# Wider token blocks, and a state product in whole float32

## The chip, the cores and the metric

The kernel runs on one core of one Trainium2 chip. The metric is the device time of one execution in microseconds (us). A core has five engines with queues of their own: TensorE (PE in the profile, its weight loads PEld) multiplies matrices into PSUM; VectorE (DVE), ScalarE (ACT) and GpSimd (POOL) work element by element; SyncE (SP) issues most of the transfers (DMAs).

## The reference

Attention with a decaying state, and a feed-forward part behind it with softplus. Inputs are float32 and random; four sequences of 768 tokens, eight heads of 64, so the feed-forward part sees 3072 tokens of 512 features, with 2048 hidden columns.

```python
for t in range(S):
    state = gamma[None, :, None, None] * state + np.einsum('bhd,bhe->bhde', k[:, :, t], v[:, :, t])
    y[:, :, t] = scale * np.einsum('bhd,bhde->bhe', q[:, :, t], state)
...
x = np.ascontiguousarray(attn_out.transpose(0, 2, 1, 3)).reshape(B * S, H * D)
h = x @ w_in
g = np.maximum(h, 0.0) + np.log1p(np.exp(-np.abs(h)))
return (g @ w_out).astype(np.float32)
```

## The kernel before

**Precision.** The code multiplies operands in two forms: float32r, one record a product in the profile, and whole float32, which the profile shows as two records a product. For most products it splits an operand into a high and a low float32r part and adds three products (high x high, high x low, low x high) in PSUM. The names end in h and l: `xh`, `xl`, `gh`, `gl`, `kh`, `kl`, and `vhl` for both parts of v.

**Attention.** It is cut into 48 units: 24 chunks of 128 tokens, each with two halves of four heads. What a unit does is spread over ticks: the dictionary `PARTS` (line 264) says at which tick after the unit's start each part runs, and a new unit begins every four ticks. `load_unit` (six ticks ahead) fetches k, q, v through SP; `decay` (two ahead) scales q and v on POOL; `operands` (0) transposes k and q on TensorE (lines 125, 127) and splits k, q and v; `scores` (2) multiplies them; `new_state` (3) multiplies k by v into `pp` and adds that to the state `td` (lines 202, 204), unless the chunk is the last of its sequence; `stack_and_outputs` (5) copies the state and makes the outputs `yp`, then `xh` and `xl`. The first ten units (`n < WHOLE`) use whole float32 products, the others the split form. For `pp` that is one product for each head on line 191 (four heads, 64 stationary and 64 moving columns), or two on lines 195 (128 moving columns) and 196. TensorE's attention results share three PSUM banks in rotation (`ps_a`, tag `a`).

**Feed-forward.** Blocks of `T` = 256 tokens. A step takes one block and two of the 16 column tiles of 128: `hidden` (lines 279 to 288) makes `hp` with 2 x 12 products of 256 columns; `softplus_1` and `softplus_2` turn that into `gh` and `gl` with two operations on VectorE, two on ScalarE and one on POOL; `second`, two steps later (`LAG`), multiplies by `w_out` into one accumulator for each 128 tokens (`acc0`, `acc1`), three products of 512 columns for each column tile and accumulator. A block has eight steps, and its accumulators are copied out at its end.

**Order.** The main loop (line 410) runs over the steps: hidden products of step s, some ticks of attention, output products of step s - 2, some more ticks. `plan` spreads the ticks that the next block needs evenly over the steps of the present one. The first blocks are special (`turns`): five steps of block 0, all of block 1, then the rest of block 0, while the weights are still being fetched and converted (`convert_weights`, with PSUM tile `wp` and buffer `w`); block 2's ticks run in the five steps ahead of it. Tile sizes its pools from the names and tags, and a planner may set independent instructions of one engine in another order than the code's.

Of the kernel before, what the change touches and what calls it, by code (L numbers as in the profile page):

```python
# [18 lines left out]
C = 128  # L19
T = 256  # L20
AHEAD = 2
# [9 lines left out]
def decay_attention_then_softplus_ffn(ctx: ExitStack, tc: tile.TileContext, q, k, v, w_in, w_out, qtab, vtab, gtab, out):  # L31
# [5 lines left out]
    NF = DF // P  # L37
    NP = NF // 2
    HH = H // 2
    NJ = HH // 2  # L40
    NT = T // P
# [4 lines left out]
    wts = ctx.enter_context(tc.tile_pool(name="wts", bufs=2))  # L46
    ps_h = ctx.enter_context(tc.tile_pool(name="ps_h", bufs=2, space=bass.MemoryType.PSUM))
    ps_o = ctx.enter_context(tc.tile_pool(name="ps_o", bufs=1, space=bass.MemoryType.PSUM))
    ps_w = ctx.enter_context(tc.tile_pool(name="ps_w", bufs=1, space=bass.MemoryType.PSUM))
    ps_a = ctx.enter_context(tc.tile_pool(name="ps_a", bufs=3, space=bass.MemoryType.PSUM))  # L50
# [23 lines left out]
    def convert_weights(f):  # L74
# [21 lines left out]
    loads, live, state, xs = {}, {}, {}, {}  # L96
    lo, up = slice(0, D), slice(D, P)
# [22 lines left out]
    def operands(n):  # L120
# [5 lines left out]
        for j in range(NJ):  # L126
            nc.tensor.transpose(tp[:, 1, j, :], qn[:, 2 * j:2 * j + 2, :], ident)  # L127
        if n < WHOLE:
            kw = attn.tile([P, NJ, C], F32, name="kw", tag="kh")
# [4 lines left out]
            live[n] = [(kw, qw), kn, vn]  # L134
            return
# [11 lines left out]
        nc.vector.tensor_tensor(vhl[:, :, 1, :], vn, vhl[:, :, 0, :].bitcast(F32), op=ALU.subtract)  # L147
        kh = kl = None
        if c < NC - 1:
            kh = attn.tile([P, HH, D], F32R, name="kh", tag="kh")  # L150
            kl = attn.tile([P, HH, D], F32R, name="kl")
            nc.scalar.copy(kh, kn)
            nc.vector.tensor_tensor(kl, kn, kh.bitcast(F32), op=ALU.subtract)
        live[n] = [kq, vhl, kh, kl]

# [26 lines left out]
    def new_state(n):  # L182
        b, c, hf = units[n]
        live[n].append(state[hf][0] if c else None)
        if c == NC - 1:
            return
        pp = ps_a.tile([D, HH, 2, D], F32, name="pp", tag="a")
        if n < WHOLE:
            kn, vn = live[n][1:3]
            for h in range(HH):  # L190
                nc.tensor.matmul(pp[:, h, 0, :], lhsT=kn[:, h, :], rhs=vn[:, h, :], start=True, stop=True)
        else:
            vhl, kh, kl = live[n][1:4]
            for h in range(HH):
                nc.tensor.matmul(pp[:, h], lhsT=kh[:, h, :], rhs=vhl[:, h], start=True, stop=False)  # L195
                nc.tensor.matmul(pp[:, h, 0, :], lhsT=kl[:, h, :], rhs=vhl[:, h, 0, :], start=False, stop=True)
        if c == 0:
            td = attn.tile([D, HH, D], F32, name=f"td{hf}")
            nc.vector.tensor_copy(td, pp[:, :, 0, :])
# [27 lines left out]
    def outputs(n):  # L227
        b, c, hf = units[n]
        kq, *rest, st = live.pop(n)
        i, off = divmod((n // 2) * C, T)  # L230
        if i not in xs:
            xs[i] = [ffn.tile([P, ND, T], F32R, name=nm) for nm in ("xh", "xl")]
        xh, xl = xs[i]
        yp = ps_a.tile([D, 2, NJ, C], F32, name="yp", tag="a")
        for j in range(NJ):
            for par in range(2):
# [7 lines left out]
                if n < WHOLE:  # L244
                    kn, vn, a = rest
                    nc.tensor.matmul(o, lhsT=vn[:, h, :], rhs=a[:, h, :], start=c == 0, stop=True)  # L246
                else:
                    vhl, kh, kl, ah, al = rest
                    nc.tensor.matmul(o, lhsT=vhl[:, h, 0, :], rhs=ah[:, h, :], start=c == 0, stop=False)  # L249
# [18 lines left out]
    per_block = PERIOD * 2 * NT  # L268

# [9 lines left out]
    def hidden(s):  # L279
        i, p = steps[s]  # L280
# [10 lines left out]
    def softplus_1(s):  # L291
        sp = sps[s] = ffn.tile([P, 2, T], F32, name="sp")
        nc.vector.tensor_scalar(sp.bitcast(U32), hps[s].bitcast(U32), 0x80000000, None, op0=ALU.bitwise_or)  # L293
        nc.scalar.activation(sp, sp, AF.Softplus)  # L294

    def softplus_2(s):
        g = sps[s]
        nc.vector.scalar_tensor_tensor(g, hps.pop(s), 0.0, g, op0=ALU.max, op1=ALU.add)  # L298
        gh = ffn.tile([P, 2, T], F32R, name="gh")
        nc.scalar.copy(gh, g)  # L300
        gl = ffn.tile([P, 2, T], F32R, name="gl")
        nc.gpsimd.tensor_tensor(gl, sps.pop(s), gh.bitcast(F32), op=ALU.subtract)  # L302
        gs[s] = gh, gl

    def second(s):
        i, p = steps[s]
        gh, gl = gs.pop(s)
        begins = s == 0 or steps[s - 1][0] != i
        ends = s + 1 == len(steps) or steps[s + 1][0] != i
        if begins:  # L310
            acc[i] = [ps_o.tile([P, DM], F32, name=f"acc{t}") for t in range(NT)]
        for k in range(2):
            wt = wout[2 * p + k]
            for t in range(NT):
                ts = slice(t * P, (t + 1) * P)
                nc.tensor.matmul(acc[i][t], lhsT=gh[:, k, ts], rhs=wt[:, 0], start=begins and k == 0, stop=False)  # L316
                nc.tensor.matmul(acc[i][t], lhsT=gh[:, k, ts], rhs=wt[:, 1], start=False, stop=False)  # L317
                nc.tensor.matmul(acc[i][t], lhsT=gl[:, k, ts], rhs=wt[:, 0], start=False, stop=ends and k == 1)  # L318
        if not ends:
            return  # L320
        for t in range(NT):
            if p < NP - 1:
# [3 lines left out]
            o = ffn.tile([P, DM], F32, name="o")  # L326
            if (i, t) in part:
                nc.vector.tensor_tensor(o, acc[i][t], part.pop((i, t)), op=ALU.add)
            else:
                (nc.scalar.copy if t % 2 else nc.vector.tensor_copy)(o, acc[i][t])  # L330
            nc.sync.dma_start(out[i * T + t * P:i * T + (t + 1) * P, :], o)

    turns = [(0, 0, TURN), (1, 0, NP), (0, TURN, NP)]
    turns += [(i, 0, NP) for i in range(2, B * S // T)]
    steps = [(i, p) for i, a, b in turns for p in range(a, b)]

    def ticks_for(i):

        return min(per_block * (i + 1) + max(PARTS) - PERIOD + 1 + AHEAD, last_tick + 1)

# [37 lines left out]

    starts = [s for s, (i, p) in enumerate(steps) if p == 0]
    plan = [0] * len(steps)
# [26 lines left out]

    for s, (i, p) in enumerate(steps):  # L410
        convert_to(2 * p + 2)
        stages(s, plan[s])
        convert_to(2 * max(p + 1, s + 1 if s < TURN else TURN + (s - TURN) // 2) + EARLY)
    for s in range(len(steps), len(steps) + LAG):
# [31 lines left out]
```

## Time and profile before

| | us |
|---|---|
| median of 3 runs | 701.77 (700.23 to 701.84) |
| profiled execution | 700.03 |
| its span, first to last instruction | 698.2 |
| TensorE busy | 684.4 |
| VectorE busy | 433.2 |
| ScalarE busy | 372.1 |
| GpSimd busy | 281.4 |

A row of a group reads: line, engine, operation, output<-inputs, shapes, xcount | busy us, mean ns of one | idle us of the engine just ahead of them, and what ended it. A row of the timeline is start, length, engine, line, operation. A matmul's length runs from its first column to a modelled end in PSUM, so the next one starts long before it ends; how fast TensorE works is read from one start to the next. A whole float32 product shows as two records.

### The profile page before, as it was taken

The page shows a single profiled execution, that of the slowest core. Times are in us where ns is not written, and L with a number is a line of the kernel's source. Part 1 is how long each engine was busy: PE and PEld are TensorE (multiplying, and loading weights), DVE is VectorE, ACT ScalarE, POOL GpSimd, SP SyncE. Part 2 cuts the span into 40 slices and gives each one's busy share as a digit, 9 for nine tenths or more (in the row PEclk, how much of TensorE's full clock was granted, in tenths as well). Part 3 has the DMA queues.
Part 4 walks back from the last instruction along what each step waited for, and adds up shares of the span by engine and source line. Part 5 has one row for each costly group of instructions (what it writes and reads, how often), then busy time and mean ns, then how long its engine had stood idle before and what let it go on. Part 6 is the DMA issues. An engine that isn't in the chain of part 4 may idle for free.

```text
span 698.2 us, 13537 instructions
## 1 busy us (share of the span) xinstructions
PE 684.4 (98%) x5056; PEld 621.3 (89%) x5056; DVE 433.2 (62%) x893; ACT 372.1 (53%) x835; POOL 281.4 (40%) x324
## 2 busy tenths in 40 slices
PE   6899999999999999999999999999999999999997
PEld 4688889899999999999999999999999999999996
DVE  4676785557666766557667666647766676544221
ACT  6988885446556546445555555445555544543221
POOL 5676667334343342343334333433433333222221
PEclk9999999999999999999999999999999999999999
DMA  9976650122112112111111111211211110000000
GB/s 266 287 201 173 192 159 1 31 61 69 31 23 69 31 25 61 31 31 54 39 23 37 49 38 24 61 37 25 62 24 39 54 31 16 31 1 1 31 1 30
DMA packets 90752, 42.82 MB, mean 61 GB/s; under 512 B 77376, under 2 KB 85568, under 8 KB 90688
## 3 DMA queue, kind: packets, MB, share of 16 engines
q1 hardware_dynamic: 90240, 41.96, 22.2%
q8 instruction: 40, 0.66, 0.4%
q14 instruction: 24, 0.20, 0.1%
q10 hardware_dynamic: 448, 0.01, 0.0%
HBM read 35.66 MB, written 6.29 MB: 60 GB/s over the span
## 4 chain that ended last, share of the span: by engine, by line
PE 96%; ACT 1%; issue 0%; DVE 0%; ACTq 0%
PE hp L286 14%; PE hp L287 13%; PE hp L288 13%; PE acc L316 13%; PE acc L317 13%; PE acc L318 13%; PE sc L171 3%; PE tp L125 1%; PE tp L127 1%; PE pp L195 1%; PE yp L250 1%; PE yp L251 1%; PE yp L249 1%; PE yp L246 1%; PE yp L240 1%; PE yp L243 1%
## 5 line engine op out<-in xcount | busy, mean ns | idle before, releaser
L286 PE MATMUL hp<-xh,winhl 128*128 128x256 f32 x768 | 221.4, 289 | 0.4 <-ACT xh L255 0.4
L288 PE MATMUL hp<-xh,winhl 128*128 128x256 f32 x768 | 217.9, 284 | 0.0
L287 PE MATMUL hp<-xl,winhl 128*128 128x256 f32 x768 | 217.6, 283 | 0.0
L302 POOL TENSOR_TENSOR gl<-sp,gh 128x512 fp32r<-128x512 f32 x96 | 125.4, 1306 | 149.3 <-ACT gh L300 86.7
L316 PE MATMUL acc<-wouthl,gh 128*128 128x512 f32 x384 | 154.3, 402 | 0.0
L317 PE MATMUL acc<-wouthl,gh 128*128 128x512 f32 x384 | 150.4, 392 | 0.0
L318 PE MATMUL acc<-wouthl,gl 128*128 128x512 f32 x384 | 149.1, 390 | 0.0
L286 PEld LDWEIGHTS hp<-xh,winhl 128*128 128x128 f32 x768 | 146.5, 191 | 2.8 <-issue 0.5
L287 PEld LDWEIGHTS hp<-xl,winhl 128*128 128x128 f32 x768 | 147.0, 191 | 1.6 <-issue 0.5
L288 PEld LDWEIGHTS hp<-xh,winhl 128*128 128x128 f32 x768 | 146.8, 191 | 0.6 <-issue 0.3
L293 DVE TENSOR_SCALAR sp<-hp 128x512 uint32<-128x512 uint32 x96 | 66.1, 690 | 70.6 <-PE hp L288 61.0
L300 ACT CAST gh<-sp 128x512 fp32r<-128x512 f32 x96 | 59.5, 620 | 74.1 <-PE acc L317 57.4
L117 POOL TENSOR_TENSOR qn<-qn,qtabs 128x256 f32<-128x256 f32 x48 | 29.4, 613 | 151.1 <-DMA qn<-in_q_dram 125.0
L294 ACT ACTIVATE sp<-sp 128x512 f32<-128x512 f32 x96 | 60.9, 634 | 49.0 <-DVE sp L293 48.7
L318 PEld LDWEIGHTS acc<-wouthl,gl 128*128 128x128 f32 x384 | 71.9, 188 | 15.6
L316 PEld LDWEIGHTS acc<-wouthl,gh 128*128 128x128 f32 x384 | 72.4, 189 | 12.5 <-issue 0.5
L317 PEld LDWEIGHTS acc<-wouthl,gh 128*128 128x128 f32 x384 | 72.5, 189 | 11.4
L298 DVE SCALAR_TENSOR_TENSOR sp<-hp,sp 128x512 f32<-128x512 f32 x96 | 65.9, 687 | 12.8 <-ACT sp L294 11.6
L142 DVE TENSOR_TENSOR kq<-tp,kq 64x256 fp32r<-64x256 f32 x76 | 32.1, 422 | 67.0 <-ACT kq L140 65.8
L139 ACT CAST kq<-tp 64x512 fp32r<-64x512 f32 x76 | 44.1, 581 | 40.0 <-PE tp L127 38.8
L255 ACT CAST xh<-yp 64x256 fp32r<-64x256 f32 x96 | 35.1, 366 | 51.0 <-PE yp L251 44.5
L257 DVE TENSOR_TENSOR xl<-yp,xh 64x256 fp32r<-64x256 f32 x96 | 39.9, 416 | 33.7 <-ACT xh L255 32.7
(85 smaller groups left out, 1082.6 us busy)
## 6 DMA issues: line engine op xcount, KB each, us to landing
win<-in_moe_w_in_dram SPq DMA_DIRECT2D x16, 512.0 KB, 4.5
wout<-in_moe_w_out_dram SPq DMA_DIRECT2D x16, 512.0 KB, 4.4
kn<-in_k_dram SPq DMA_DIRECT2D x48, 128.0 KB, 2.3
qn<-in_q_dram SPq DMA_DIRECT2D x48, 128.0 KB, 2.8
vn<-in_v_dram SPq DMA_DIRECT2D x48, 128.0 KB, 2.2
out_dram<-o SPq DMA_DIRECT2D x24, 256.0 KB, 2.1
gtab_sb<-in_gtab_dram ACTq DMA_DIRECT2D x2, 2.0 KB, 3.8
qtabs<-in_qtab_dram ACTq DMA_DIRECT2D x1, 4.0 KB, 2.4
```

What stands on the lines that cost most here:

```text
L139: nc.scalar.copy(kq[own, :2, par], tp[own])
L286: nc.tensor.matmul(hp[:, k], lhsT=wt[:, 0, d, :], rhs=xh[:, d, :], start=d == 0, stop=False)
L287: nc.tensor.matmul(hp[:, k], lhsT=wt[:, 0, d, :], rhs=xl[:, d, :], start=False, stop=False)
L288: nc.tensor.matmul(hp[:, k], lhsT=wt[:, 1, d, :], rhs=xh[:, d, :], start=False, stop=d == ND - 1)
L293: nc.vector.tensor_scalar(sp.bitcast(U32), hps[s].bitcast(U32), 0x80000000, None, op0=ALU.bitwise_or)
L294: nc.scalar.activation(sp, sp, AF.Softplus)
L298: nc.vector.scalar_tensor_tensor(g, hps.pop(s), 0.0, g, op0=ALU.max, op1=ALU.add)
L300: nc.scalar.copy(gh, g)
L302: nc.gpsimd.tensor_tensor(gl, sps.pop(s), gh.bitcast(F32), op=ALU.subtract)
L316: nc.tensor.matmul(acc[i][t], lhsT=gh[:, k, ts], rhs=wt[:, 0], start=begins and k == 0, stop=False)
L317: nc.tensor.matmul(acc[i][t], lhsT=gh[:, k, ts], rhs=wt[:, 1], start=False, stop=False)
L318: nc.tensor.matmul(acc[i][t], lhsT=gl[:, k, ts], rhs=wt[:, 0], start=False, stop=ends and k == 1)
```

## The change

The blocks have 256, 256, six times 384 and 256 tokens. A step takes as many column tiles as fit 512 columns of `hp`: two for a block of 256, as before, and one for a block of 384, which then has 16 steps and three accumulators. PSUM's bank for the third accumulator is the one that the weights' conversion had for `wp` alone; `w` shares the buffers of the output tile `o`. The state's product `pp` is made from whole float32 k and v in every unit, right behind the transposes (tick 0) and no longer at tick 3; `kh`, `kl`, their two operations and the second addition to the state are gone. k and q have two buffers for three, v keeps three.

```diff
-T = 256
+BLOCKS = (256, 256) + 6 * (384,) + (256,)
+WIDE = 512
...
-            wp = ps_w.tile([P, n], U32, name="wp")
-            w = wts.tile([P, n], U32, name="w")
+            wp = ps_o.tile([P, n], U32, name="wp", tag="acc2")
+            w = ffn.tile([P, n], U32, name="w", tag="o")
...
-            t = attn.tile([P, HH, D], F32, name=nm, bufs=3)
+            t = attn.tile([P, HH, D], F32, name=nm, bufs=3 if nm == "vn" else 2)
...
+        if c < NC - 1:
+            pp[n] = ps_a.tile([D, HH, D], F32, name="pp", tag="a")
+            for h in range(HH):
+                nc.tensor.matmul(pp[n][:, h, :], lhsT=kn[:, h, :], rhs=vn[:, h, :], start=True, stop=True)
...
-        kh = kl = None
-        if c < NC - 1:
-            kh = attn.tile([P, HH, D], F32R, name="kh", tag="kh")
-            kl = attn.tile([P, HH, D], F32R, name="kl")
-            nc.scalar.copy(kh, kn)
-            nc.vector.tensor_tensor(kl, kn, kh.bitcast(F32), op=ALU.subtract)
-        live[n] = [kq, vhl, kh, kl]
+        live[n] = [kq, vhl]
...
-        pp = ps_a.tile([D, HH, 2, D], F32, name="pp", tag="a")
-        if n < WHOLE:
-            kn, vn = live[n][1:3]
-            for h in range(HH):
-                nc.tensor.matmul(pp[:, h, 0, :], lhsT=kn[:, h, :], rhs=vn[:, h, :], start=True, stop=True)
-        else:
-            vhl, kh, kl = live[n][1:4]
-            for h in range(HH):
-                nc.tensor.matmul(pp[:, h], lhsT=kh[:, h, :], rhs=vhl[:, h], start=True, stop=False)
-                nc.tensor.matmul(pp[:, h, 0, :], lhsT=kl[:, h, :], rhs=vhl[:, h, 0, :], start=False, stop=True)
...
-            nc.vector.tensor_tensor(td, pp[:, :, 0, :], td, op=ALU.add)
-        if n >= WHOLE:
-            nc.vector.tensor_tensor(td, pp[:, :, 1, :], td, op=ALU.add)
+            nc.vector.tensor_tensor(td, pp.pop(n), td, op=ALU.add)
...
+    def operands_and_state(n):
+        operands(n)
+        new_state(n)
...
-    PARTS = {-6: load_unit, -2: decay, 0: operands, 2: scores, 3: new_state, 5: stack_and_outputs}
+    PARTS = {-6: load_unit, -2: decay, 0: operands_and_state, 2: scores, 5: stack_and_outputs}
...
-        hp = hps[s] = ps_h.tile([P, 2, T], F32, name="hp")
-        for k in range(2):
-            wt = win[2 * p + k].rearrange("p t (c f) -> p t c f", c=ND)
+        hp = hps[s] = ps_h.tile([P, len(fs), BLOCKS[i]], F32, name="hp", tag="hp")
+        for k, f in enumerate(fs):
+            wt = win[f].rearrange("p t (c f) -> p t c f", c=ND)
...
-    turns = [(0, 0, TURN), (1, 0, NP), (0, TURN, NP)]
-    turns += [(i, 0, NP) for i in range(2, B * S // T)]
-    steps = [(i, p) for i, a, b in turns for p in range(a, b)]
+    turns = [(0, 0, 2 * TURN), (1, 0, NF), (0, 2 * TURN, NF)]
+    turns += [(i, 0, NF) for i in range(2, len(BLOCKS))]
+    steps = []
+    for i, a, b in turns:
+        m = WIDE // BLOCKS[i]
+        steps += [(i, tuple(range(f, f + m))) for f in range(a, b, m)]
```

More of the change, by code (lines that the diff above doesn't have):

```diff
@@ L38, in decay_attention_then_softplus_ffn @@
     NP = NF // 2
+    assert sum(BLOCKS) == B * S
+    FIRST = np.cumsum((0,) + BLOCKS)
     HH = H // 2
     NJ = HH // 2
-    NT = T // P
     const = ctx.enter_context(tc.tile_pool(name="const", bufs=1))
@@ L95, in decay_attention_then_softplus_ffn @@
     units = [(c // NC, c % NC, hf) for c in range(B * NC) for hf in range(2)]
-    loads, live, state, xs = {}, {}, {}, {}
+    loads, live, pp, prior, state, xs = {}, {}, {}, {}, {}, {}
     lo, up = slice(0, D), slice(D, P)
@@ L228, in outputs @@
         b, c, hf = units[n]
-        kq, *rest, st = live.pop(n)
-        i, off = divmod((n // 2) * C, T)
+        kq, *rest = live.pop(n)
+        st = prior.pop(n)
+        token = (n // 2) * C
+        i = int(np.searchsorted(FIRST, token, "right")) - 1
+        off = token - FIRST[i]
         if i not in xs:
-            xs[i] = [ffn.tile([P, ND, T], F32R, name=nm) for nm in ("xh", "xl")]
+            xs[i] = [ffn.tile([P, ND, BLOCKS[i]], F32R, name=nm, tag=nm) for nm in ("xh", "xl")]
         xh, xl = xs[i]
@@ L244, in outputs @@
                 if n < WHOLE:
-                    kn, vn, a = rest
+                    vn, a = rest
                     nc.tensor.matmul(o, lhsT=vn[:, h, :], rhs=a[:, h, :], start=c == 0, stop=True)
                 else:
-                    vhl, kh, kl, ah, al = rest
+                    vhl, ah, al = rest
                     nc.tensor.matmul(o, lhsT=vhl[:, h, 0, :], rhs=ah[:, h, :], start=c == 0, stop=False)
@@ L279, in hidden @@
     def hidden(s):
-        i, p = steps[s]
+        i, fs = steps[s]
         xh, xl = xs[i]
-        hp = hps[s] = ps_h.tile([P, 2, T], F32, name="hp")
-        for k in range(2):
-            wt = win[2 * p + k].rearrange("p t (c f) -> p t c f", c=ND)
+        hp = hps[s] = ps_h.tile([P, len(fs), BLOCKS[i]], F32, name="hp", tag="hp")
+        for k, f in enumerate(fs):
+            wt = win[f].rearrange("p t (c f) -> p t c f", c=ND)
             for d in range(ND):
@@ L291, in softplus_1 @@
     def softplus_1(s):
-        sp = sps[s] = ffn.tile([P, 2, T], F32, name="sp")
+        sp = sps[s] = ffn.tile(list(hps[s].shape), F32, name="sp", tag="sp")
         nc.vector.tensor_scalar(sp.bitcast(U32), hps[s].bitcast(U32), 0x80000000, None, op0=ALU.bitwise_or)
@@ L298, in softplus_2 @@
         nc.vector.scalar_tensor_tensor(g, hps.pop(s), 0.0, g, op0=ALU.max, op1=ALU.add)
-        gh = ffn.tile([P, 2, T], F32R, name="gh")
+        gh = ffn.tile(list(g.shape), F32R, name="gh", tag="gh")
         nc.scalar.copy(gh, g)
-        gl = ffn.tile([P, 2, T], F32R, name="gl")
+        gl = ffn.tile(list(g.shape), F32R, name="gl", tag="gl")
         nc.gpsimd.tensor_tensor(gl, sps.pop(s), gh.bitcast(F32), op=ALU.subtract)
@@ L305, in second @@
     def second(s):
-        i, p = steps[s]
+        i, fs = steps[s]
+        NT = BLOCKS[i] // P
         gh, gl = gs.pop(s)
@@ L310, in second @@
         if begins:
-            acc[i] = [ps_o.tile([P, DM], F32, name=f"acc{t}") for t in range(NT)]
-        for k in range(2):
-            wt = wout[2 * p + k]
+            acc[i] = [ps_o.tile([P, DM], F32, name=f"acc{t}", tag=f"acc{t}") for t in range(NT)]
+        for k, f in enumerate(fs):
+            wt = wout[f]
             for t in range(NT):
@@ L317, in second @@
                 nc.tensor.matmul(acc[i][t], lhsT=gh[:, k, ts], rhs=wt[:, 1], start=False, stop=False)
-                nc.tensor.matmul(acc[i][t], lhsT=gl[:, k, ts], rhs=wt[:, 0], start=False, stop=ends and k == 1)
+                nc.tensor.matmul(acc[i][t], lhsT=gl[:, k, ts], rhs=wt[:, 0], start=False, stop=ends and f == fs[-1])
         if not ends:
@@ L321, in second @@
         for t in range(NT):
-            if p < NP - 1:
+            if fs[-1] < NF - 1:
                 part[i, t] = ffn.tile([P, DM], F32, name="part")
@@ L325, in second @@
                 continue
-            o = ffn.tile([P, DM], F32, name="o")
+            o = ffn.tile([P, DM], F32, name="o", tag="o")
             if (i, t) in part:
@@ L379, in decay_attention_then_softplus_ffn @@
             loaded += 1
-    starts = [s for s, (i, p) in enumerate(steps) if p == 0]
+    starts = [s for s, (i, fs) in enumerate(steps) if fs[0] == 0]
     plan = [0] * len(steps)
@@ L408, in stages @@
             done += 1
-    for s, (i, p) in enumerate(steps):
-        convert_to(2 * p + 2)
+    for s, (i, fs) in enumerate(steps):
+        convert_to(fs[-1] + 1)
         stages(s, plan[s])
-        convert_to(2 * max(p + 1, s + 1 if s < TURN else TURN + (s - TURN) // 2) + EARLY)
+        convert_to(2 * max(fs[-1] // 2 + 1, s + 1 if s < TURN else TURN + (s - TURN) // 2) + EARLY)
     for s in range(len(steps), len(steps) + LAG):
```

15 lines of the change are left out of this document (6 added, 9 removed).

## The prediction

> **What bounds the kernel now.** I read the page's first, second and fourth part, then the busy time in three stretches.
>
> ```profile
> span 698.2 us, 13537 instructions
> ...
> PE 684.4 (98%) x5056; PEld 621.3 (89%) x5056; DVE 433.2 (62%) x893; ACT 372.1 (53%) x835; POOL 281.4 (40%) x324
> ...
> PE 96%; ACT 1%; issue 0%; DVE 0%; ACTq 0%
> ```
> ```profile
> 0.00:28.00 28.00, 18.27 (x114) 13.82 (x115) 14.45 (x36) 20.11 (x44) 17.19 (x32) 1.00 1.04 282
> 28.00:644.00 616.00, 616.00 (x4637) 562.61 (x4636) 405.61 (x838) 340.44 (x773) 253.60 (x284) 1.00 0.21 55
> 644.00:698.00 54.00, 50.08 (x310) 44.85 (x308) 13.16 (x20) 11.57 (x20) 10.56 (x9) 1.00 0.05 20
> ```
>
> The columns after the length are PE, PEld, DVE, ACT and POOL. From 28 to 644 us TensorE never stops, at a granted clock of 1.00, while VectorE works 406 of 616 us and ScalarE 340. The chain of waits is 96% TensorE. So an edit that only relieves another engine brings nothing there, and an edit of TensorE's stream counts in full. A busy row is no measure of that stream, because its matmuls overlap; its price is the step from one start to the next. The counts come from the groups, the steps from the timeline.
>
> ```profile
> L286 PE MATMUL hp<-xh,winhl 128*128 128x256 f32 x768 | 221.4, 289 | 0.4 <-ACT xh L255 0.4
> ...
> L316 PE MATMUL acc<-wouthl,gh 128*128 128x512 f32 x384 | 154.3, 402 | 0.0
> ...
> L195 PE MATMUL pp<-vhl,kh 128*64 128x128 f32 x120 | 17.2, 243 | 0.0
> ```
> ```profile
> 396.34 0.39 PE L318 MATMUL acc<-wouthl,gl 128*128 128x512 f32 x1
> 396.56 0.22 PE L195 MATMUL pp<-vhl,kh 128*64 128x128 f32 x1
> ...
> 397.00 0.36 PE L286 MATMUL hp<-xh,winhl 128*128 128x256 f32 x1
> 397.20 0.28 PE L287 MATMUL hp<-xl,winhl 128*128 128x256 f32 x1
> ...
> 399.83 0.28 PE L288 MATMUL hp<-xh,winhl 128*128 128x256 f32 x1
> 399.95 0.38 PE L125 MATMUL tp<-ident,kn 128*128 128x128 f32 x2
> ...
> 400.63 0.39 PE L317 MATMUL acc<-wouthl,gh 128*128 128x512 f32 x1
> 400.86 0.39 PE L318 MATMUL acc<-wouthl,gl 128*128 128x512 f32 x1
> ...
> 402.92 0.39 PE L318 MATMUL acc<-wouthl,gl 128*128 128x512 f32 x1
> ```
>
> Lines 286 and 316 are each the first of three that the code issues together, with the same count. In the second fence a row is start, length, engine, line. A step's 24 hidden products start at 397.00; from the second (397.20) to the last (399.83) are 22 steps: 2.63 / 22 = 0.1195 us for 256 columns. Of the 12 output products of 512 columns, the third starts at 400.86 and the last at 402.92: 2.06 / 9 = 0.2289 us.
>
> **Part 1, the wider blocks.** A block takes 16 x 12 = 192 hidden products whatever its width (3 x 768 = 2304 for twelve blocks). Six blocks of 384 take the place of nine of 256, so 1728 products of 256 columns become 1152 of 384. The output products stay 1152 of 512 columns, three to each 128 tokens and column tile. No row has 384 columns. Halfway between the two steps measured is 0.1742 us, which I take, because the width is halfway too. Bounds: at the rate per column of 512 it is 0.75 x 0.2289 = 0.1717, at that of 256 it is 1.5 x 0.1195 = 0.1793. Before: 1728 x 0.1195 = 206.5 us; after: 1152 x 0.1742 = 200.7. **Saved 5.8 us**, between 8.7 (0.1717) and 0 (0.1793).
>
> **Part 2, the state's product.** Lines 195 and 196 go: 120 / 4 heads = 30 units. Without them 396.34 to 397.20 would hold one step of 512 and one of 256 columns, so a unit's eight products cost 0.86 - 0.23 - 0.12 = 0.51 us. In their place comes the whole float32 form that ten early units use (line 191: eight records a unit, two passes a head).
>
> ```profile
> 33.07 0.68 PE L191 MATMUL pp<-vn,kn 128*64 128x64 f32 x8
> 33.68 0.51 PE L286 MATMUL hp<-xh,winhl 128*128 128x256 f32 x2
> 34.02 0.28 PE L287 MATMUL hp<-xl,winhl 128*128 128x256 f32 x1
> ```
> ```profile
> 36.05 0.38 PE L125 MATMUL tp<-ident,kn 128*128 128x128 f32 x2
> 36.27 0.38 PE L127 MATMUL tp<-ident,qn 128*128 128x128 f32 x2
> 36.59 0.43 PE L240 MATMUL yp<-qw,st 128*64 128x128 f32 x2
> 36.95 0.38 PE L287 MATMUL hp<-xl,winhl 128*128 128x256 f32 x1
> 37.17 0.28 PE L288 MATMUL hp<-xh,winhl 128*128 128x256 f32 x1
> ```
>
> The eight passes last 33.07 to 33.68, 0.61 us. The two hidden products behind them take 0.34 instead of 0.24: 0.10 more, as again at 36.95 (0.22 instead of 0.12). Ahead of such a group there is a pause too: two transposes take 0.22 (36.05 to 36.27), the next two 0.32, because a float32 product with 64 stationary columns follows, and after the change the state's product stands right behind the transposes. Together 0.61 + 0.10 + 0.10 = 0.81 us against 0.51. The transposes now pay 0.80 - 0.12 - 0.23 = 0.45 (399.83 to 400.63), four times 0.11 and 0.01, so 0.01 comes off: 0.29 us more a unit, x 30 = **8.7 us added**. The ten early units have the form and its two pauses already; there it only moves.
>
> By the Trainium skill (TensorEngine Tiling (Array Packing), Key Properties) a change of tiling mode drains TensorE. That speaks against this part. The trace agrees for the whole float32 form alone: the 64-column group at 396.56 starts 0.22 us behind a 512-column product, with no pause.
>
> **Part 3, what goes from the other engines.**
>
> ```profile
> L153 DVE TENSOR_TENSOR kl<-kn,kh 128x256 fp32r<-128x256 f32 x30 | 29.1, 970 | 0.5
> ...
> L152 ACT CAST kh<-kn 128x256 fp32r<-128x256 f32 x30 | 12.2, 408 | 6.8 <-PE pp L196 3.9 <-issue 2.0
> ...
> L330 DVE COPY o<-acc 128x512 f32<-128x512 f32 x11 | 7.5, 683 | 6.0 <-PE acc L318 6.0
> ```
>
> VectorE loses 29.1 us here and 30 second additions to the state, ScalarE 12.2. The softplus work falls on 96 tiles of 384 instead of 72 of 512: the same columns and 24 more fixed parts for each operation. All of it lies beside TensorE's 616 full us, so I cost it at nothing in both directions.
>
> **Part 4, queues and buffers.** The unit's k and q have two buffers for three, so SP's next load of k waits for the state's product, and what is queued behind it on SP (q, v) waits too. 44 of the 48 units are worked off in the 616 us, one in 14 us, and such a load lands in 2.3 us:
>
> ```profile
> kn<-in_k_dram SPq DMA_DIRECT2D x48, 128.0 KB, 2.3
> ```
> ```profile
> 403.89 0.43 DVE L143 TENSOR_TENSOR kq<-tp,kq 64x256 fp32r<-64x256 f32 x1
> ```
>
> Nothing, then; without that cover a late unit costs at most those 2.3 us. The weights' conversion now shares the third accumulator's bank; it belongs to the first two blocks, which leave that bank empty: nothing. At a block's end VectorE copies out two accumulators and not one, 2 x 0.68 = 1.4 us; the next block's first output product comes 12 hidden products (2.1 us) later, and that hides it. Uncovered it would be 0.7 us at each of six ends, 4 in all. One place is tighter: block 2's 24 ticks must fit in five steps, where 16 did. Once, a unit's scores then stand behind its own transposes with only 0.81 us of state products and 16 output passes (at the 0.11 of a transpose, also 128 columns; 1.76) between, 2.6 us, while the key and query pairs are ready 4.37 - 0.45 = 3.9 us after the transposes end (399.95 to 404.32). That may stop TensorE for up to 1.3 us, unless the planner sets feed-forward products between. I take nothing and keep 1.3 for the range.
>
> **The sum.** -5.8 + 8.7 = +2.9 us. The profiled execution took 700.03 us (span 698.2 and 1.8 around it), so it becomes 702.9. The median of the runs shown, 701.77 (700.23 to 701.84), lies 1.7 higher; I forecast against it: **704.7 us**. A measurement of this kernel can tell about 0.3%, 2.1 us, from no change; the forecast is 0.4%.
>
> **Rivals.** *B, 384 columns run at the rate of 512.* The step is 0.1717 to 0.1735, the saving 8.7 to 6.6, the change 0 to +2.1: 701.8 to 703.9, no difference that can be told. For it: the fixed part of a step need not grow with its columns. Against: halfway is 0.1742.
>
> *C, columns cost the same at 384 as at 256.* The step is 0.177 to 0.1793, the saving 2.6 to 0: +6.1 to +8.7, 707.9 to 710.5. For it: 0.1195 for 256 columns may be a rate and not a sum with a fixed part. Against: 512 columns take 0.229, not 0.239. By the Trainium skill (TensorE: Matmul & The Clock Gate, Back-to-back issue gap) a step is the columns at 2.4 GHz and 2.5 ns; by that 576 fewer products save an estimated 1.5 us and the change is +7.2, also here. Both steps measured here are longer than that rule gives (0.1195 against 0.109, 0.2289 against 0.216).
>
> *D, the pauses are not paid* (the other side). From 36.05 to 37.17 are 1.12 us; four transposes and the two passes at 0.11 and one hidden step of 0.12 make 0.78, so the pauses of one group come to 0.34. Without them a group costs 0.81 - 0.34 = 0.47 and part 2 saves 30 x 0.05 = 1.5: -7.3, 694.5 us. Place: the 30 units behind unit ten. It decides the sign that can be told if the pauses shrink below 0.17 a unit (30 x 0.12 = 3.7, and 3.7 - 5.8 = -2.1). For it: the rows with a pause are from the early stage alone. Against: TensorE is busy throughout at 33 and 36 us and pauses all the same, and the old form's rows show none. By the Trainium skill (TensorEngine Tiling (Array Packing), When to Use Tiling) column tiling belongs to every stationary side of at most 64 columns; by that the old form would have paid as well and the change would save too, which the row at 396.56 contradicts.
>
> *E, block 2's crowding stops TensorE* more than once: 1.3 us for each of some three units, +4 on top: 708.6.
>
> **Chances.** Forecast (step 0.1735 to 0.177, +2.1 to +6.1, 703.9 to 707.9) 0.47; B 0.27; C 0.10; D 0.12; E 0.04. Slower: 0.47 + 0.10 + 0.04 = 0.61; same 0.27; faster 0.12. The range leaves out D and the upper part of C: 701.0 (B's end and the scatter of the runs, 0.8) to 709.5.
>
> **What would show it.** Right: hidden products of 384 columns start 0.174 us apart; a state product takes eight passes in 0.61 us with 0.10 lost on either side; the stretch from 28 us to the last attention product is still without a gap; VectorE falls by some 30 us and the time does not follow. Wrong: steps under 0.172 or over 0.177; no longer step behind the state's product; gaps in TensorE around block 2's start, or at a block's end, where three accumulators and not two must be copied out before the next block's first output product.

## The result, and the profile after

| | before | after |
|---|---|---|
| median of the runs, us | 701.67 (700.23 to 701.84) | 708.41 (708.10 to 709.56) |
| profiled execution, us | 700.03 | 708.59 |
| last product starts at, us of the span | 693.7 | 702.6 |

The changed kernel is slower: ratio 1.0104 (95% interval 1.0086 to 1.0121), some 7.3 us. The direction was forecast and the time lies inside the range, but the forecast was +2.9 us. From the page of the changed kernel, its first, second and fourth part:

```profile
span 706.9 us, 12409 instructions
...
PE 687.9 (97%) x4480; PEld 618.9 (88%) x4480; DVE 409.3 (58%) x884; ACT 366.4 (52%) x850; POOL 282.9 (40%) x348
...
PEclk8899999999999999999999999999999999999999
...
PE 92%; ACT 2%; DVE 2%; issue 1%; DMA 1%; POOL 1%; SPq 0%; POOLq 0%; DVEq 0%; ACTq 0%
```

The busy time in stretches (window, length, then PE, PEld, DVE, ACT, POOL, the granted clock):

```profile
0.00:28.00 28.00, 16.05 (x92) 13.01 (x93) 14.11 (x36) 20.45 (x44) 16.73 (x31) 0.84 1.01 281
28.00:644.00 616.00, 612.88 (x4022) 552.71 (x4021) 378.93 (x824) 331.43 (x782) 252.86 (x307) 1.00 0.21 54
...
157.00:172.00 15.00, 12.47 (x110) 10.50 (x110) 13.06 (x34) 10.69 (x30) 4.96 (x8) 1.00 0.41 107
```

Before, TensorE had no gap from 28 to 644 us, and its chain share was 96%. Now the chain gives 4% to ScalarE and VectorE, and the long stretch holds 3.1 us without TensorE. 2.5 us of that lie in the 15 us from 157 on, where VectorE works 13.1 us of 15. Block 2 starts at 159.5 us. The stops themselves, from the timeline of TensorE (start, length, and in brackets the idle time ahead and who ended it):

```profile
159.49 0.62 PE L279 MATMUL hp<-xh,winhl 128*128 128x384 f32 x2 [0.42 <-ACT xh L245]
160.41 0.41 PE L125 MATMUL tp<-ident,kn 128*128 128x128 f32 x2 [0.31 <-issue]
...
164.93 0.48 PE L170 MATMUL sc<-kq 128*128 128x256 f32 x2 [0.67 <-DVE kq L148]
...
168.65 0.65 PE L132 MATMUL pp<-vn,kn 128*64 128x64 f32 x8 [0.15 <-DVE al L174]
...
170.41 0.27 PE L240 MATMUL yp<-al,vhl 128*64 128x128 f32 x1 [0.59 <-POOL al L176]
...
172.01 0.59 PE L170 MATMUL sc<-kq 128*128 128x256 f32 x3 [0.21 <-DVE kq L148]
```

Five of these six rows name a step of the attention chain: twice the key and query pairs (`kq`) for the scores, once the masked scores (`al`, line 176) for the outputs, once the first columns of block 2 (`xh`), and once line 174, the last reader of a score tile. There `pp` presumably waits for its bank, since it shares three banks with the score tiles and reads none of them. The row at 160.41 names no engine. The steps that the forecast priced stand in the same timeline:

```profile
401.03 0.38 PE L127 MATMUL tp<-ident,qn 128*128 128x128 f32 x2
401.34 0.68 PE L132 MATMUL pp<-vn,kn 128*64 128x64 f32 x8
401.95 0.44 PE L279 MATMUL hp<-xh,winhl 128*128 128x384 f32 x1
402.23 0.34 PE L280 MATMUL hp<-xl,winhl 128*128 128x384 f32 x1
402.40 0.34 PE L281 MATMUL hp<-xh,winhl 128*128 128x384 f32 x1
...
403.97 0.33 PE L281 MATMUL hp<-xh,winhl 128*128 128x384 f32 x1
```

From 402.23 to 403.97 are ten steps of 384 columns: 0.174 us each. The two transposes ahead of `pp` take 0.31 us instead of 0.22, its eight passes 0.61 (401.34 to 401.95), and the first hidden step behind it 0.28 instead of 0.17. At the start TensorE now waits for v (the second row):

```profile
22.83 0.44 PE L127 MATMUL tp<-ident,qn 128*128 128x128 f32 x2 [0.40 <-POOL qn L117]
26.41 1.11 PE L132 MATMUL pp<-vn,kn 128*64 128x64 f32 x8 [3.14 <-POOL vn L118]
...
31.89 0.51 PE L279 MATMUL hp<-xh,winhl 128*128 128x256 f32 x2 [0.18 <-ACT xh L245]
```

Before, the first hidden product started at 27.7 us. A part of these 4.2 us is made up: block 1's first output copy on VectorE starts 2.5 us later than before.

```profile
140.35 0.68 DVE L330 COPY o<-acc 128x512 f32<-128x512 f32 x1
```
```profile
142.81 0.68 DVE L324 COPY o<-acc 128x512 f32<-128x512 f32 x1
```

**Where the time went.** I went through every product of the traces, from one start to the next, and counted each at the undisturbed step of its kind (0.1196 us for 256 columns, 0.1742 for 384, 0.058 for a pass of `pp`, and so on). What a step takes beyond that is a pause if it stands beside a group of 64 stationary columns. It is a stop where it is more than 0.16 us (0.19 beside `pp`). e1 and e8 are experiments below: e1 has twelve blocks of 256, e8 has three of 256 and then six of 384, both with the new state product.

| us, profiled executions | before | after | e1 | e8 |
|---|---|---|---|---|
| hidden products, steps | 275.6 | 269.6 | 275.6 | 269.6 |
| state product, steps and pauses | 18.6 + 5.1 | 18.7 + 13.3 | 18.7 + 12.3 | 18.7 + 12.6 |
| stops up to 50 us | 9.4 | 12.2 | 14.1 | 12.9 |
| stops from 140 to 185 us | 0 | 3.9 | 0 | 0 |
| later stops | 0 | 0 | 0 | 0.6 |
| all else, by difference | 381.4 | 381.3 | 379.2 | 381.0 |
| first to last product | 690.1 | 699.0 | 699.9 | 695.4 |

So +8.9 us from first to last product is -6.0 (wider blocks) + 8.3 (state product) + 2.8 (start) + 3.9 (block 2) - 0.1 (all else). By the medians it is less, since the profiled execution of before lies 1.6 us under its median.

### The profile page after: what moved, and what is told of

It reads as the page before. It is cut to its first block, busy times and chain, and to the rows that moved or that the text cites. A ratio compares the mean times of both kernels' runs of the same rounds, so it can differ in the third digit from the quotient of the medians.

```text
span 706.9 us, 12409 instructions
## 1 busy us (share of the span) xinstructions
PE 687.9 (97%) x4480; PEld 618.9 (88%) x4480; DVE 409.3 (58%) x884; ACT 366.4 (52%) x850; POOL 282.9 (40%) x348
## 4 chain that ended last, share of the span: by engine, by line
PE 92%; ACT 2%; DVE 2%; issue 1%; DMA 1%; POOL 1%; SPq 0%; POOLq 0%; DVEq 0%; ACTq 0%
PE acc L310 13%; PE hp L279 13%; PE acc L311 13%; PE hp L281 13%; PE hp L280 13%; PE acc L312 12%; PE pp L132 3%; PE sc L170 3%; PE tp L127 1%; PE yp L239 1%; PE tp L125 1%; PE yp L241 1%; PE yp L240 1%; PE yp L232 1%; PE yp L233 1%
## 5 line engine op out<-in xcount | busy, mean ns | idle before, releaser
L295 POOL TENSOR_TENSOR gl<-sp,gh 128x384 fp32r<-128x384 f32 (+1 forms) x120 | 128.7, 1073 | 188.8 <-ACT gh L293 150.4
L279 PE MATMUL hp<-xh,winhl 128*128 128x384 f32 (+1 forms) x576 | 185.5, 323 | 0.6 <-ACT xh L245 0.6
L280 PE MATMUL hp<-xl,winhl 128*128 128x384 f32 (+1 forms) x576 | 183.9, 319 | 0.2 <-DVE xl L247 0.2
L281 PE MATMUL hp<-xh,winhl 128*128 128x384 f32 (+1 forms) x576 | 183.8, 319 | 0.0
L286 DVE TENSOR_SCALAR sp<-hp 128x384 uint32<-128x384 uint32 (+1 forms) x120 | 69.8, 582 | 138.2 <-PE hp L281 129.7
L287 ACT ACTIVATE sp<-sp 128x384 f32<-128x384 f32 (+1 forms) x120 | 65.5, 547 | 114.3 <-DVE sp L286 114.0
L279 PEld LDWEIGHTS hp<-xh,winhl 128*128 128x128 f32 x576 | 108.6, 189 | 5.4 <-ACT xh L245 1.0
L280 PEld LDWEIGHTS hp<-xl,winhl 128*128 128x128 f32 x576 | 108.9, 189 | 4.3 <-DVE xl L247 0.7
L293 ACT CAST gh<-sp 128x384 fp32r<-128x384 f32 (+1 forms) x120 | 64.0, 534 | 89.0 <-PE acc L311 46.8
L281 PEld LDWEIGHTS hp<-xh,winhl 128*128 128x128 f32 x576 | 108.8, 189 | 0.6 <-issue 0.2
L291 DVE SCALAR_TENSOR_TENSOR sp<-hp,sp 128x384 f32<-128x384 f32 (+1 forms) x120 | 69.6, 582 | 33.8 <-ACT sp L287 32.8
L310 PEld LDWEIGHTS acc<-wouthl,gh 128*128 128x128 f32 x384 | 72.3, 188 | 12.3 <-issue 0.9
L176 POOL TENSOR_SCALAR_AFFINE_SELECT ah<-ah 128x512 fp32r<-128x512 f32 (+1 forms) x48 | 30.4, 634 | 47.2 <-DVE al L173 39.1
```

Source lines behind the costliest of these rows:

```text
L279: nc.tensor.matmul(hp[:, k], lhsT=wt[:, 0, d, :], rhs=xh[:, d, :], start=d == 0, stop=False)
L280: nc.tensor.matmul(hp[:, k], lhsT=wt[:, 0, d, :], rhs=xl[:, d, :], start=False, stop=False)
L281: nc.tensor.matmul(hp[:, k], lhsT=wt[:, 1, d, :], rhs=xh[:, d, :], start=False, stop=d == ND - 1)
```

## The experiments

The theory after the result: the state product costs what was forecast, the wider blocks save what was forecast, and the crowding of block 2's 24 ticks into five steps takes most of that saving back. Rivals: 384 columns are no cheaper; the pause does not come from the 64 columns; the start (v awaited at tick 0, fewer buffers) is what is missing. The ratios below are each to the runs of before on the same chip beside them, whose median was 700.0 to 701.9 us.

**e1, the state product alone.** The blocks go back to 256.

```diff
-BLOCKS = (256, 256) + 6 * (384,) + (256,)
+BLOCKS = 12 * (256,)
```


> The second part of the change alone: twelve blocks of 256 tokens as before, the state's product in whole float32 behind the transposes. Theory (pauses around a float32 product with 64 stationary columns, 0.29 us a unit net, and a later start): 30 x 0.29 = 8.7 and 1 to 2 us at the start, 710 to 713 us against 701.7 before. Rival (the pauses cost nothing in the full stretch, the time is lost by the wider blocks): 701 to 704 us.

Measured: 708.97 us, ratio 1.0119 [1.0101, 1.0137], +8.3 us. The 710 to 713 us expected were missed, but the kernel before ran at 700.1 beside it and not at 701.7. The 8.3 is not part 2 alone: by the table e1 pays 7.3 us for the state product and 4.7 at the start, and has 2.2 less in all else. The changed kernel's ratio is lower by 1 us, inside both intervals: its six wide blocks bring nothing that can be told, where 5.8 us were forecast. Block 2 is without a stop here (busy time, columns as above):

```profile
150.00:175.00 25.00, 25.00 (x191) 22.82 (x190) 17.75 (x39) 13.24 (x33) 10.28 (x13) 1.00 0.20 55
```

**e2, the wide blocks alone.** The blocks of the change, with the old state product at tick 3.

```diff
-            pp[n] = ps_a.tile([D, HH, D], F32, name="pp", tag="a")
...
+            kh = attn.tile([P, HH, D], F32R, name="kh", tag="kh")
+            kl = attn.tile([P, HH, D], F32R, name="kl")
...
+        pp = ps_a.tile([D, HH, 2, D], F32, name="pp", tag="a")
...
-    PARTS = {-6: load_unit, -2: decay, 0: operands_and_state, 2: scores, 5: stack_and_outputs}
+    PARTS = {-6: load_unit, -2: decay, 0: operands, 2: scores, 3: new_state, 5: stack_and_outputs}
```


> The first part alone: blocks of 384 as in the change, the state's product split and at tick 3 as before (v has two buffers for three, which the memory asks for). Theory: 1152 x 0.174 for 1728 x 0.1195, 6 us saved, less 2 to 4 us of stops in TensorE where block 2's 24 ticks crowd into five steps: 697 to 700 us. Rival 1 (the crowding costs nothing): 695.5 to 696.5. Rival 2 (wider blocks lose time elsewhere, by 24 more steps and three accumulators to copy out): 702 to 705.

Measured: 710.53 us, ratio 1.0136 [1.0112, 1.0160], a clear miss. The hidden steps fall to the same 269.6 us and the pauses of `pp` stay near before's, but from 140 to 185 us the stops come to 9.9 us, and some 4 us more lie in stretched hidden steps. The timeline of TensorE shows why they cost so much:

```profile
156.91 0.22 PE L257 MATMUL yp<-ah,vhl 128*64 128x128 f32 x1
159.19 0.62 PE L295 MATMUL hp<-xh,winhl 128*128 128x384 f32 x2 [2.06 <-ACT xh L261]
...
162.49 0.52 PE L297 MATMUL hp<-xh,winhl 128*128 128x384 f32 x1
...
165.05 0.52 PE L297 MATMUL hp<-xh,winhl 128*128 128x384 f32 x1
```
```profile
162.00:166.00 4.00, 4.00 (x15) 3.90 (x15) 2.61 (x8) 1.20 (x4) 1.91 (x3) 0.50 0.15 35
```

Behind a stop of 2.06 us the granted clock is 0.50, and eight steps of 384 columns take 2.56 us (162.49 to 165.05), 0.32 each instead of 0.174. The same happens behind stops of 1.89 us at 169 us and 1.53 us at 179 us. So the wide blocks stop TensorE at block 2 with the old state product as well, and harder. Why harder was not separated: this kernel has both the operations that the change removed from VectorE and ScalarE and two buffers for each of k, q and v.

**e3, e15 and e16, the spread of block 2's ticks.** e3 gives them eight steps, e15 eleven. e16 goes the other way on e1's narrow blocks: 16 ticks in three steps.

```diff
-            a = b - TURN
+            a = b - 8
```
```diff
-            a = b - TURN
+            a = b - 11
```
```diff
-BLOCKS = (256, 256) + 6 * (384,) + (256,)
+BLOCKS = 12 * (256,)
...
-            a = b - TURN
+            a = b - 3
```


> The changed kernel with block 2's 24 ticks spread over eight steps and not five, three a step as before the change. Theory (stops between 128 and 180 us cost 3.9 us of the profiled execution): 704 to 705.5 us against 708.4. Rival (the stops are made up later, and the loss is in the pauses alone): 708 to 709.

> The changed kernel with block 2's 24 ticks spread over eleven steps in place of five (the run with eight steps is on record). If the crowding of those ticks is what stops TensorE at 158 to 172 us, the stops (3.9 us in the changed kernel, 2.4 with eight steps) fall below 1.5 us and the ratio to the kernel before to 1.004 to 1.008. If block 2's width itself is the cause (three chunks of tokens must be ready at once, whatever the spread), 2.4 us or more stay and the ratio is 1.009 to 1.011.

> The twelve blocks of 256 with the whole float32 state product (1.0119 on record, no stops at block 2), but block 2's 16 ticks in three steps in place of five: 5.3 ticks a step against 4.8 in the changed kernel. If ticks for each step are what stops TensorE, stops of 3 us or more appear at 140 to 165 us and the ratio is 1.016 to 1.020. If the stops need blocks of 384, nothing appears and the ratio stays at 1.011 to 1.013.

| | ticks a step | stops from 140 to 185 us | ratio |
|---|---|---|---|
| changed kernel | 24 in 5 | 3.9 | 1.0104 [1.0086, 1.0121] |
| e3 | 24 in 8 | 2.4 | 1.0096 [1.0077, 1.0114] |
| e15 | 24 in 11 | 1.7 | 1.0064 [1.0047, 1.0080] |
| e1 | 16 in 5 | 0 | 1.0119 [1.0101, 1.0137] |
| e16 | 16 in 3 | 2.7 | 1.0151 [1.0130, 1.0172] |

The window of e1 that had no gap, now in e16, and after it the same window of e15:

```profile
150.00:175.00 25.00, 23.22 (x171) 20.91 (x169) 17.20 (x40) 13.39 (x33) 9.17 (x12) 0.93 0.23 59
```
```profile
150.00:175.00 25.00, 24.02 (x155) 20.80 (x155) 18.81 (x45) 12.73 (x33) 10.40 (x14) 1.00 0.20 55
```

More ticks a step bring stops into narrow blocks too; fewer take them out of wide ones. Both moved the way the crowding theory says. The sizes were smaller than expected: e15 kept 1.7 us where under 1.5 was expected, e16 got 2.7 where 3 was, and its ratio lies under the 1.016 expected. e3 missed its 704 to 705.5 us with 707.37, and its ratio cannot be told from the changed kernel's; of the two wide ones, e15 alone shows the gain in its time. The number of ticks a step is not all of it: e3's 24 in eight steps leave 2.4 us, while e8's, below, leave none, and e15 still stops at 2.2 ticks a step, where e1 at 3.2 does not.

How full VectorE is does not tell these kernels apart either. In the 15 us from 157 on it works 13.06 us in the changed kernel, with stops. In e14, described below, which has a block 2 of 256, it works 13.60 us and TensorE never stops; in e16 it works 11.09, and TensorE stops:

```profile
157.00:172.00 15.00, 15.00 (x111) 13.96 (x110) 13.60 (x30) 9.42 (x24) 6.89 (x8) 1.00 0.28 75
157.00:172.00 15.00, 13.37 (x97) 12.36 (x97) 11.09 (x27) 6.98 (x19) 5.97 (x8) 0.89 0.19 44
```

So VectorE's load alone is not the cause. That leaves how the links of the units' chains fall due one behind the other, which is argued from the named waits and was not varied by itself.

**e8, the wide blocks one block later.**

```diff
-BLOCKS = (256, 256) + 6 * (384,) + (256,)
+BLOCKS = 3 * (256,) + 6 * (384,)
```


> The changed kernel with blocks of three times 256 and six times 384: block 2 has 256 tokens, so 16 ticks and not 24 stand in its five steps, and the block of 256 at the end is gone. Theory: the stops of 3.9 us between 155 and 172 us go, 704 to 705.5 us. Rival 1 (they are made up later): 708 to 709. Rival 2 (stops move to block 3's start, which needs 24 ticks in eight steps): 706 to 708.

Measured: 707.24 us, ratio 1.0097 [1.0082, 1.0112]. Block 2 is narrow, the first wide block has eight steps ahead of it, and the stops are gone (150 to 175 us):

```profile
150.00:175.00 25.00, 25.00 (x193) 22.92 (x192) 19.51 (x42) 13.57 (x34) 10.21 (x13) 1.00 0.20 54
```

The last product starts at 698.85 us instead of 702.62, 3.8 us earlier, about the 3.9 us of stops. But now the last block is wide, and from its last product to the end of the span are 6.65 us instead of 4.3. So only part of it reached the time: the 704 to 705.5 us expected were missed, and the ratio cannot be told from the changed kernel's. The time is in the range of rival 2, but the stops did not move to block 3; one of 0.6 us stands ahead of the last block.

**e4, the pause of the state product.** Two heads go into one product of 128 stationary and 128 moving columns. Of each such product only the two squares where a head meets itself are used; the other half of the work is thrown away. The edit shown leaves out that the state is then added and copied in this layout, with two additions for one on VectorE and one copy less on ScalarE.

```diff
-            pp[n] = ps_a.tile([D, HH, D], F32, name="pp", tag="a")
-            for h in range(HH):
-                nc.tensor.matmul(pp[n][:, h, :], lhsT=kn[:, h, :], rhs=vn[:, h, :], start=True, stop=True)
+            pp[n] = ps_a.tile([P, NJ, P], F32, name="pp", tag="a")
+            for j in range(NJ):
+                two = slice(2 * j, 2 * j + 2)
+                nc.tensor.matmul(pp[n][:, j, :], lhsT=kn[:, two, :], rhs=vn[:, two, :], start=True, stop=True)
```


> The changed kernel with the state's product made for two heads at once: 128 stationary and 128 moving columns in whole float32, of which the two diagonal quarters are used; four passes a unit of 0.112 us for eight of 0.058. Theory (the pause belongs to the 64 stationary columns): 0.45 us and no pause for 0.46 and 0.35, 0.36 a unit, 11 us with the early ones less some that already share theirs: 697 to 700 us. Rival (the pause belongs to whole float32, or to the wait in front of it): within 1 us of 708.4.

Measured: 699.91 us, ratio 0.9993 [0.9982, 1.0004]. One unit of it in the timeline:

```profile
395.95 0.38 PE L127 MATMUL tp<-ident,qn 128*128 128x128 f32 x2
396.17 0.61 PE L133 MATMUL pp<-vn,kn 128*128 128x128 f32 x4
396.54 0.42 PE L279 MATMUL hp<-xh,winhl 128*128 128x384 f32 x1
396.80 0.34 PE L280 MATMUL hp<-xl,winhl 128*128 128x384 f32 x1
```

The transposes take their plain 0.22 us. The passes and the hidden step behind them take 0.63 together (396.17 to 396.80); four plain passes of 0.11 and a step of 0.17 make 0.61, so there is no pause behind the group either. From the second pair of transposes to the second hidden product are 0.85 us, against 1.20 in the changed kernel (401.03 to 402.23). The pauses of the state product fall from 13.3 to 2.7 us, though the stops at block 2 stay (4.3 us). So the pause belongs to the 64 stationary columns of the whole float32 form; e4 also doubles the moving columns, but the row at 36.59 us in the prediction has 128 of those with 64 stationary ones, and it pauses. By the Trainium skill (TensorEngine Tiling (Array Packing), The Problem) the full array is underused with a side of at most 64. The measurement agrees: four passes that fill the array, with half of their work thrown away, take 0.37 us, the eight passes of 64 columns 0.61.

**e5, e11 and e12, the start and the buffers.** e5 is the changed kernel with the state product of the ten early units back at tick 3. e11 is e1 with three buffers for k and q. e12 is e1 with both.

```diff
-        if c < NC - 1:
+        if c < NC - 1 and n >= WHOLE:
...
+    def early_state(n):
+        if n < WHOLE:
+            new_state(n)
...
-    PARTS = {-6: load_unit, -2: decay, 0: operands_and_state, 2: scores, 5: stack_and_outputs}
+    PARTS = {-6: load_unit, -2: decay, 0: operands_and_state, 2: scores, 3: early_state, 5: stack_and_outputs}
```
```diff
-            t = attn.tile([P, HH, D], F32, name=nm, bufs=3 if nm == "vn" else 2)
+            t = attn.tile([P, HH, D], F32, name=nm, bufs=3)
```


> The changed kernel with the state's product of the ten early units back at tick 3, behind the scores; the others stay behind the transposes. Theory (at the start TensorE stands in front of the product until GpSimd has scaled v, 3.3 us before the first hidden product): the first hidden product starts near 28 us and not at 31.9, and 1.5 to 4 us are won, 704.5 to 707 us. Rival (the early stretch is set by the weights' conversion, and what is lost at the start is regained by 130 us): 708 to 709.

> The second part alone (blocks of 256), with three buffers for k and q again. Theory A (the start is late because two buffers hold the loads of k and q back behind the state's product): first hidden product near 28 us and not 31.9, 705.5 to 707.5 us against 709.0. Theory B (because the product stands in front of the scores and waits for v): as with two buffers, 708.5 to 709.5.

> The same, and the early units' state product back at tick 3: the start is then that of the kernel before, but for the buffers that the weights' conversion shares. Theory (buffers and place together make the later start): first hidden product at 27.5 to 28.5 us, 30 x 0.29 over the kernel before and no more, 707 to 709 us. Rival (the conversion's shared buffers make it): first hidden product still at 30 us or later.

Measured: e5 709.64 us, 1.0135 [1.0118, 1.0152]; e11 708.75 us, 1.0102 [1.0084, 1.0120]; e12 709.28 us, 1.0108 [1.0092, 1.0124]. e5 is no faster than the changed kernel (704.5 to 707 us were expected), and e11 and e12 are level with e1. In e12 the first hidden product starts at 28.9 us, in e11 at 32.5; the last product starts at 703.1 us in both. e12's stops are 2.7 us less than e11's, but its pauses beside groups of 64 columns are 2.9 more. In e5 the first hidden product still starts at 31.1 us and not near 28. The wait for v is gone, but TensorE, with two buffers for k, now waits for a load of k:

```profile
22.82 0.66 PE L126 MATMUL tp<-ident,kn 128*128 128x128 f32 x2 [2.04 <-DMA kn<-in_k_dram]
```

e12, with three, has no such wait. So the early wait for v can be removed, but no time comes of it, and by the times of e11 and e13 the buffers cost nothing that can be told.

**e10, e13, e9 and e14, what the pairs are worth.** All have e4's product and e5's tick for the early units. e10 has blocks of 256, e13 the same with three buffers for k and q, e9 the blocks of e8, and e14 wide blocks in the middle alone:

```diff
-BLOCKS = (256, 256) + 6 * (384,) + (256,)
+BLOCKS = 3 * (256,) + 4 * (384,) + 3 * (256,)
```


> The same with twelve blocks of 256 tokens: what the wider blocks are worth when nothing else is lost. Theory: 6 us more than with the blocks of 384, and 3 us less than before the change (the state's products cost 20.7 us in place of 23.7): 697 to 699 us. Rival (the wider blocks bring nothing once the stops are gone): the same time as with them, within 1.5 us.

> Blocks of 256, the state's products for two heads at once, early ones at tick 3, three buffers for k and q. Theory A (buffers): 1.5 to 3 us below the same with two buffers (695.7), 692.5 to 694.5. Theory B: within 1 us of 695.7.

> All three together: state's products for two heads at once, those of the early units at tick 3, blocks of three times 256 and six times 384. Theory: from the 699.9 us of the pairs alone the stops at block 2 (4.3 us by its trace) and most of the 3.8 us at the start go, 692 to 695 us, below both kernels. Rival (the stops are not additive with the pauses): 697 to 700.

> State's products for two heads at once, early ones at tick 3, two buffers; three blocks of 256, four of 384, three of 256. Theory: four of the wider blocks save 4.0 us of TensorE, without block 2's crowding and without the longer end of a last block of 384: 691.5 to 693.5 us against 695.7 with twelve blocks of 256. Rival (every change of width stops TensorE, as the 0.6 us ahead of the last block of 384 did): 694 to 697.

| | us | ratio |
|---|---|---|
| e10, narrow | 695.70 | 0.9934 [0.9920, 0.9949] |
| e13, narrow, three buffers | 696.69 | 0.9933 [0.9915, 0.9950] |
| e9, wide at the end | 696.83 | 0.9949 [0.9932, 0.9966] |
| e14, wide in the middle | 695.64 | 0.9911 [0.9896, 0.9927] |

All four beat both kernels. e14 has the lowest ratio, though its interval overlaps that of e10. Its last product starts at 687.9 us, e10's at 690.3; by the steps, four wide blocks in place of six narrow ones should save 4 us. Most expectations failed here: e10 was expected behind e9 by 6 us and is 1 us ahead of it, within the 1.5 us of its rival; e9 lies over its 692 to 695 us, and e14 over its 691.5 to 693.5, in the range of its rival (its trace has 0.9 us of stops, at 201 and 220 us). e13 is level with e10, so three buffers bring nothing. That the wider blocks pay at all is therefore not shown by any time here; at best e14's ratio points that way. As in e8, wide blocks at the very end (e9) lose at the tail: 6.65 us from the last product to the end of the span, against 4.3 in e10.

## Why the prediction was wrong in size

**Part 1 was right as a price.** The step of 384 columns is 0.174 us, so rivals B and C fall, and the hidden products take 6.0 us less, against 5.8. The measured 708.41 us lies in C's range, but not for C's reason.

**Part 2 was right.** The forecast was 8.7 us, the traces give 8.3 for the changed kernel and 7.3 for e1. That e1's time is also longer by 8.3 us is in part chance, since it holds the start as well. Rival D falls as it was put: the pauses are paid. But e4 takes them away in another form. e10's 695.7 us is close to D's 694.5 by chance: D's sum holds 5.8 us from wider blocks, and e10 has none.

**Part 3 held in the long stretch only.** VectorE fell by 24 us (433.2 to 409.3), not by 30, and the time did not follow. But "beside TensorE's 616 full us" is no cover at block 2, where TensorE waits for VectorE, ScalarE and GpSimd. Whether e2's larger stops come from these operations was not tried by itself.

**Part 4 is the step that failed:** "I take nothing and keep 1.3 for the range" for block 2's 24 ticks in five steps. The runs show 3.9 us of stops there. The working looked at one unit's scores behind its own transposes, and gave TensorE that one wait once. The trace has five named waits in 13 us, for `kq`, for `al`, for `xh`. With nearly five ticks a step several units hang on the engines beside TensorE at once, and each link of the chain from transposes to outputs can come late. Rival E had the mechanism and the size (about 4 us) and was given a chance of 0.04; the traces of e8, e15 and e16 bear it out. That its 708.6 us meets the measured 708.41 is in part luck, since it left out the start. The mean of the long stretch, VectorE's 406 of 616 us, did not show the crowded place, and e14's 13.60 of 15 us shows that a mean over the place itself would not have either.

**The start was not in the sum at all.** "There it only moves" overlooked that at tick 0 `pp` waits for v (3.14 us on line 118), and the stops up to 50 us grew by 2.8. e5 and e12 show that undoing the move brings nothing, so this wait is not by itself the price; what else makes the early stage longer in the changed kernel stays open. The clock may have a part: from 12.6 to 19 us it was 0.50, against 1.00 before. But a clock of 1.00 at the very start is not to be taken at its word. The view gives 1.00 for the first 12.5 us of before, and there, at 7.32 us, the eight passes of `pp` take 1.04 us to the next product and not 0.61. How much of the later start the clock makes was not separated.

**The rest held.** No stop of the changed kernel waits for `wp` or `w`, and the three accumulators at a block's end show none: after 185 us there is no stop at all. The two buffers for k and q cost no time that can be told (e11, e13), though in e5 a load of k came 2.04 us late, near the 2.3 that part 4 named for a late unit.

**What stays open.** Why 24 ticks in eight steps stop TensorE ahead of block 2 (e3, 2.4 us) and not ahead of block 3 (e8, none), and why 24 in eleven still do (e15, 1.7 us). Something in a wide block 2 itself, or in its place behind the early stage, has a part that no run separates from the ticks.

## What to carry to other kernels

A wider tile saves its fixed parts all through the kernel, but it also asks for more finished input at its first use: price the stretch ahead of that first use by following the chain of the units that stand in it at once, link by link. Busy time, of the whole or of the stretch, does not tell whether a link comes late. A product is not priced by its columns alone: look in the timeline at the steps before and behind its group, and try the full-width form even if half of it is thrown away. Place the wide tiles where the work ahead of them is spread and the tail behind them is short.

## What the runs showed of the hardware

Whole float32 products with 64 stationary columns pause beside their group (0.31 for 0.22 us ahead, 0.28 for 0.17 in the hidden step behind); with 128 stationary columns there is no pause on either side (0.22 ahead; 0.63 for 0.61 with the step behind). A stop of TensorE can cost more than its length: behind stops of 2.06, 1.89 and 1.53 us in e2 and of 1.20 us in e16 the granted clock fell to 0.50, while the 0.81 us in e3 and the stops of up to 0.7 us at block 2 in the changed kernel left it at 1.00. e16:

```profile
158.92 0.39 PE L280 MATMUL hp<-xl,winhl 128*128 128x256 f32 x1 [1.20 <-DVE xl L247]
160.00:163.00 3.00, 3.00 (x16) 3.00 (x16) 1.34 (x3) 0.00 (x0) 1.27 (x2) 0.50 0.00 0
```

The length alone does not decide. In e1 the same wait for v as in the changed kernel, 3.13 us against 3.14, left the clock at 1.00: its eight passes, with the drawn-out end of the last, take 0.68 us, those of the changed kernel 1.11 at 26.41 us (the clock from 27 to 29 us is 1.00 in e1 and 0.50 there).

```profile
26.63 0.68 PE L132 MATMUL pp<-vn,kn 128*64 128x64 f32 x8 [3.13 <-POOL vn L118]
```

By the Trainium skill (TensorE: Matmul & The Clock Gate, Part 1: The HAM clock gate) the clock is halved after an idle window of about 3.4 us. The 0.50 agrees with the halving, but here it followed idle stretches of 1.20 to 2.06 us, and one of 3.13 us was not followed by it.
